# Attention stage: the bonus summed on TensorE, the gate in groups of four, and two ScalarE steps moved

## The chip, the cores and the metric

The kernel runs on one core of a Trainium2 chip. The metric is the device time of one execution in microseconds; times are given as the median of several runs, and one further execution was profiled.

## The reference

The program is a chain of three parts. Only the first is touched. It is linear attention with a decaying state and a bonus for the current token, for 4 batches, 8 heads, 768 tokens and a head width of 48:

```python
for t in range(S):
    kt, vt, rt = (k[:, :, t], v[:, :, t], r[:, :, t])
    cur = np.einsum('bhd,bhe->bhde', u[None] * kt, vt)
    y[:, :, t] = np.einsum('bhd,bhde->bhe', rt, state + cur)
    state = w[None, :, :, None] * state + np.einsum('bhd,bhe->bhde', kt, vt)
```

The term with `cur` is the bonus: for each token and head it is the number sum over d of r·u·k, times the row v. The 3072 rows of 384 values that come out are then multiplied by `w_gate` (384 x 8); these logits send each row to one of 8 experts with room for 384 rows each, by the order of all logits. Each expert applies two matrices, and a last part takes the maximum of three products and one more matrix.

## The kernel before

The attention is cut into 24 steps, one for each chunk of 128 tokens of one batch: step i works on batch i % 4 and chunk i // 4, so the state of a batch is needed again four steps later. The loop in `run` (L318 to L344) issues, for each i, the work of several steps at different distances, and every engine takes its own part of that order strictly in sequence:

- SP issues the loads of step i+4 (`load`: k, r and v in rows of tokens) and of step i+3 (`across`: r turned, as `rt`), and the store of the rows of step i-1.
- POOL multiplies `rt` by powers of the decay (`decayed`, L128), k by inverse powers (`natural`, L183, result `kp`), makes r·k and then r·k·u (`bonus`, L191 and L192, result `rk`), and after DVE has summed that over d (`extra`, L200, result `bon`) multiplies v by the sums (L202, result `bv`).
- PE turns `kp` of step i+2 (`turn`, L212, into the one buffer `pT`), multiplies it with `rt` for step i+1 (`scores`, L226, into `pA`), turns the output rows of step i-1 (`cross`, L297, into `pX`), runs four products of constants whose result nobody reads (`keep`, L236), forms the output of step i from the state and from the masked scores (`rows`, L247, into `pY`), multiplies the turned rows of step i-2 by the gate (`gate`, L307, into `lg`, where all logits stay until the loop ends), and forms the new state (`state`, L281, into `pK`).
- DVE masks the scores (L229, `am`), adds `bv` to the output (L262, `x`) and adds the old state (L285, `st`).
- ScalarE copies `pT` out (L214, `kt`) and `pX` (L299, `xt`), squares the rows of step i for a later scale (L263), and copies the new state back with its decay, in four instructions (L289, `S`).

Between these, at the places `side(1)` to `side(4)`, the loop runs items of a feed: pieces of preparing later weights, each a few instructions on DVE and ScalarE (squares L610, splits L677 and L681, bit work L717 to L748, splits L773 and L776), now and then a small product on PE. How many run at a place follows from fixed costs written in the code, and that list does not depend on the time. When the 24 steps are done, the logits are copied out (L352), and the routing begins with them.

Of the kernel before, what the change touches and what calls it, by code (L numbers as in the profile page):

```python
# [37 lines left out]
KEEP = 4  # L38
# [6 lines left out]
class Attention:  # L45


    def __init__(self, ctx, tc, K, r, rt, k, v, w, u, wg, x_dram, spare, routing):
        self.spare, self.routing = spare, routing
        self.tc, self.nc, self.K = tc, tc.nc, K  # L50
        self.r, self.rt, self.k, self.v, self.x_dram = r, rt, k, v, x_dram
# [4 lines left out]
        self.psum = ctx.enter_context(tc.tile_pool(name="psum_a", bufs=1, space=PSUM))  # L56
        self.steps = [(b, c) for c in range(NC) for b in range(B)]
        self.LD, self.RN, self.KN, self.BV, self.RT, self.KT, self.AM, self.X, self.XT, self.RK = ({} for _ in range(10))
        wcol = self.tabs.tile([128, NP], F32, name="wcol")
        nc.vector.memset(wcol, 1.0)  # L60
        for s in range(2):
            nc.sync.dma_start(wcol[HALF[s]], ap(w, s * D, [[1, D], [R2, NP]]))
        self.RB, self.KB, self.KP = ([self.tabs.tile([128, NP * C], F32, name=f"{name}{j}") for j in range(m)]
                                     for name, m in (("rt", 4), ("kt", 2), ("kp", 4)))
# [14 lines left out]
        self.ub = self.tabs.tile([128, DM], F32, name="ub")  # L79
        nc.sync.dma_start(self.ub, ap(u, 0, [[0, 128], [1, DM]]))  # L80
# [4 lines left out]
        self.wg = self.tabs.tile([128, 3, E], F32, name="wg")  # L85
        nc.sync.dma_start(self.wg, ap(wg, 0, [[E, 128], [128 * E, 3], [1, E]]))
# [3 lines left out]
        self.bonus(1)  # L90
        for i in range(2):
            self.decayed(i, nc.vector)
        self.bonus(0, nc.vector)
        self.fading()
        self.bank = self.psum.tile([128, 512], F32, name="lg")
        self.lg = self.bank[:, :NT * E].rearrange("p (m e) -> p m e", e=E)
        nc.tensor.matmul(self.bank[:, 256:], self.K.onesf.bitcast(BF16)[:, :128], self.K.onesf.bitcast(BF16), start=True, stop=True,
                         skip_group_check=True)
# [19 lines left out]
    def across(self, i):  # L118
# [3 lines left out]
        t = self.RT[i] = self.RB[i % 4]  # L122
# [62 lines left out]
    def bonus(self, i, engine=None):  # L185
        if i >= NT:
            return
        engine = engine or self.nc.gpsimd
        kn, rn, vn = self.LD[i]
        t = self.RK[i] = self.work.tile([128, DM], F32, name="rk")  # L190
        engine.tensor_mul(t, rn, kn)  # L191
        engine.tensor_mul(t, t, self.ub)  # L192

    def extra(self, i):
# [7 lines left out]
        nc.gpsimd.tensor_mul(bv.rearrange("p (h d) -> p h d", h=H), vn.rearrange("p (h d) -> p h d", h=H),  # L202
# [3 lines left out]
    def turn(self, i):  # L206
# [3 lines left out]
        pk = psum.tile([128, 512], F32, name="pT")  # L210
# [20 lines left out]

    def keep(self, n):

        ones = self.K.onesf.bitcast(BF16)
        for _ in range(n):
            self.nc.tensor.matmul(self.bank[:, 256:], ones[:, :128], ones, start=False, stop=True, skip_group_check=True)  # L236

    def rows(self, i):
# [24 lines left out]
        nc.scalar.activation(self.K.junk[:, :DM], x, AF.Square, accum_out=self.K.norms[:, i:i + 1])  # L263
# [7 lines left out]
    def state(self, i):  # L271
# [16 lines left out]
        for j in range(NP):  # L288
            nc.scalar.activation(S[:, j, :D], t[:, j, :D], AF.Copy, scale=self.w128[:, j:j + 1])  # L289

    def cross(self, i):
# [6 lines left out]
        xt = self.XT[i] = work.tile([128, 3, C], F32, name="xt", bufs=3)  # L298
        nc.scalar.activation(xt, px, AF.Copy)  # L299

    def gate(self, i):
        if i < 0:
            return
        b, c = self.steps[i]
        m = b * NC + c
        for j in range(3):
            self.nc.tensor.matmul(self.lg[:, m, :], self.XT[i][:, j, :], self.wg[:, j, :],  # L307
                                  start=(i == 0 and j == 0), stop=j == 2, skip_group_check=True)

    def run(self, feed):  # L310
# [40 lines left out]
        K = self.K  # L351
        nc.scalar.activation(K.raw, self.lg, AF.Copy, scale=-1.0)  # L352
# [1064 lines left out]
def body(ctx, tc, r, rt, k, v, w, u, wg, w1, w2, v1, v2, v3, wo, out, dbg=None):  # L1417
# [14 lines left out]
    with ExitStack() as actx:  # L1432
        A = Attention(actx, tc, K, r, rt, k, v, w, u, wg, x_dram,
# [11 lines left out]
_INS = ['r', 'rt', 'k', 'v', 'w', 'u', 'moe_w_gate', 'moe_w1', 'moe_w2', 'moe2_w1', 'moe2_w2', 'moe2_w3', 'moe2_w_out']  # L1445
# [3 lines left out]
def layout(inputs):  # L1449
# [5 lines left out]
    for name in _INS:  # L1455
        if name == "rt":
            a = inputs["r"].reshape(B, NP, 2, NC, C, D).transpose(0, 3, 2, 5, 1, 4)
        elif name in "rkv":
            a = inputs[name].transpose(0, 2, 1, 3)
        else:  # L1460
            a = inputs[name]
# [25 lines left out]
```

## Time and profile before

| | us |
|---|---|
| median of 3 runs (lowest, highest) | 698.33 (697.42, 699.98) |
| the profiled execution | 696.23 |
| its span, first to last instruction | 694.5 |

Over the whole span PE is busy 93%, DVE 58%, ScalarE 51% and POOL 34%. The page cuts the span in 40 slices of 17.4 us; a digit is the busy share in tenths. POOL's line is 6999999960050003..., so POOL is full from the second to the eighth slice, and this is the attention: its loop ends at 160.5 us. The granted clock of TensorE (line PEclk, tenths of full speed) is 8999999995579999: near full in the attention, lower in the routing that follows, and full in the experts.

A busy PE in these views is a modelled figure: records of products overlap, and each lasts longer than the time to the next. The distance between the starts of neighbouring groups is therefore read, not their length.

### The profile page before, as it was taken

The numbers are of one execution on the slowest core, as the hardware profiler recorded it, in microseconds if no ns is written. First come the engines' busy times: TensorE is split into PE (matmuls) and PEld (weight loads), VectorE is DVE, ScalarE is ACT, GpSimd is POOL, SyncE is SP. The second block draws the span as 40 slices with busy tenths as digits, with TensorE's granted clock in tenths as the row PEclk, the third lists the DMA queues.
The fourth block names the chain that finished last, engine by engine and source line by source line (L and its number), as shares of the span: only waits on it lengthen the run. The fifth ranks groups of instructions, "written<-read, shape, count | busy, mean of one in ns | idle before, by whom it ended". The sixth has DMA issues, their size and how long they took to land.

```text
span 694.5 us, 14402 instructions
## 1 busy us (share of the span) xinstructions
PE 644.6 (93%) x5663; PEld 427.2 (62%) x5663; DVE 400.7 (58%) x1068; ACT 351.5 (51%) x785; POOL 238.0 (34%) x264
## 2 busy tenths in 40 slices
PE   7999998996599998699999999999999999999996
PEld 5788777875476554356666656666665666666663
DVE  7778897776725867646466455644636553451321
ACT  3766657643425556367466547446365536342321
POOL 6999999960050003113022112102212111110222
PEclk8999999995579999899999999999999999999999
DMA  7996757513034516016235211620612220000000
GB/s 220 315 295 216 246 186 250 162 37 103 2 107 139 172 42 194 22 68 160 68 103 108 98 57 30 170 75 35 160 45 74 45 89 1 35 0 1 36 1 34
DMA packets 54762, 72.97 MB, mean 105 GB/s; under 512 B 21408, under 2 KB 42016, under 8 KB 54688
## 3 DMA queue, kind: packets, MB, share of 16 engines
q1 hardware_dynamic: 51616, 62.55, 29.3%
q0 software_dynamic: 3072, 9.44, 4.7%
q8 instruction: 46, 0.75, 0.5%
q14 instruction: 28, 0.23, 0.1%
HBM read 58.41 MB, written 9.44 MB: 98 GB/s over the span
## 4 chain that ended last, share of the span: by engine, by line
PE 54%; issue 8%; DVE 5%; ACT 4%; POOL 1%; POOLq 0%; DVEq 0%; ACTq 0%
PE pg L897 25%; PE ps L897 20%; PE px L990 8%; ACT w L677 1%; DVE top L972 1%; POOL gt L977 1%; ACT junk L610 1%; DVE da L739 1%; DVE x2s L953 0%; ACT gt L976 0%; DVE ht L925 0%; DVE v L776 0%; DVE sc L423 0%; DVE da L732 0%; POOL out_dram L995 0%
## 5 line engine op out<-in xcount | busy, mean ns | idle before, releaser
L897 PE MATMUL pg<-x2s,v 128*128 128x384 f16 x1296 | 218.2, 326 | 5.3 <-ACT top L970 3.2
L897 PEld LDWEIGHTS <-v 128*128 128x128 f16 x1296 | 126.6, 98 | 90.9 <-issue 6.0
L977 POOL TENSOR_TENSOR gt<-top,gt 128x384 f16<-128x384 f32 x48 | 44.5, 928 | 349.2 <-ACT gt L976 295.5
L897 PEld LDWEIGHTS <-w 128*128 128x128 f16 x1242 | 116.8, 98 | 73.7 <-issue 2.3
L681 DVE SCALAR_TENSOR_TENSOR w<-stage,sc,w 128x512 f16<-128x512 f32 (+1 forms) x80 | 70.9, 906 | 61.1 <-ACT w L677 60.9
L972 DVE SCALAR_TENSOR_TENSOR top<-pg,sc,top 128x384 f32<-128x384 f32 x96 | 59.1, 615 | 74.4 <-PE pg L897 63.6
L897 PE MATMUL ps<-ht,w 128*128 128x384 f16 x576 | 94.9, 326 | 1.6 <-DVE ht L925 1.6
L897 PE MATMUL ps<-xt,w 128*128 128x384 f16 (+1 forms) x540 | 88.4, 317 | 0.2 <-ACT xt L888 0.2
L990 PE MATMUL px<-wo,gt 128*128 128x384 f16 x432 | 75.0, 334 | 6.9 <-DVE wo L776 3.0
L976 ACT ACTIVATE gt<-top 128x384 f16<-128x384 f32 x48 | 25.1, 523 | 109.5 <-DVE top L972 109.5
L990 PEld LDWEIGHTS <-gt 128*128 128x128 f16 x432 | 42.7, 100 | 38.1 <-issue 8.8
L677 ACT ACTIVATE w<-stage,sc 128x512 f16<-128x512 f32 (+1 forms) x80 | 61.6, 798 | 2.2 <-DVE sc L461 2.2
L610 ACT ACTIVATE junk<-stage 128x768 bf16<-128x768 f32 x64 | 53.7, 838 | 0.9
L925 DVE SCALAR_TENSOR_TENSOR ht<-ps,ht 128x384 f16<-128x384 f32 x56 | 31.0, 555 | 32.1 <-ACT ht L924 32.1
L995 POOL DMA_INDIRECT out_dram<-o,ids x24 | 23.9, 996 | 46.7 <-ACT o L993 46.7
L970 ACT ACTIVATE top<-pg,sc 128x384 f32<-128x384 f32 x48 | 27.6, 576 | 20.8 <-PE pg L897 18.3
L263 ACT ACTIVATE junk<-x 128x384 bf16<-128x384 f32 x24 | 12.6, 524 | 47.0 <-DVE x L262 44.7
L936 ACT ACTIVATE x<-ps 128x384 f32<-128x384 f32 x24 | 11.7, 490 | 47.0 <-PE ps L897 47.0
L924 ACT ACTIVATE ht<-ps 128x384 f16<-128x384 f32 x56 | 26.8, 482 | 15.9 <-PE ps L897 15.7
L993 ACT ACTIVATE o<-px,sc 128x384 f32<-128x384 f32 x24 | 13.9, 580 | 38.8 <-PE px L990 35.5
L229 DVE TENSOR_TENSOR am<-pA,mask 128x512 f32<-128x512 f32 x48 | 30.7, 681 | 4.3 <-PE pA L226 4.2
L128 POOL TENSOR_TENSOR rt<-rt,tr 128x512 f32<-128x512 f32 x22 | 31.4, 1427 | 0.2 <-DMA rt<-in_rt_dram 0.2
(231 smaller groups left out, 884.3 us busy)
## 6 DMA issues: line engine op xcount, KB each, us to landing
stage<-in_moe_w_dram SPq DMA_DIRECT2D x41, 768.0 KB, 5.6
kn<-in_k_dram SPq DMA_DIRECT2D x24, 192.0 KB, 4.9
rn<-in_r_dram SPq DMA_DIRECT2D x24, 192.0 KB, 5.0
v<-in_v_dram SPq DMA_DIRECT2D x24, 192.0 KB, 4.0
rt<-in_rt_dram SPq DMA_DIRECT2D x48, 96.0 KB, 3.5
x_rows<-x SPq DMA_DIRECT2D x24, 192.0 KB, 2.9
stage<-in_moe_w_out_dram SPq DMA_DIRECT2D x3, 768.0 KB, 4.4
xg<-x_rows,ids POOLq DMA_INDIRECT x24, 4.6
```

The costliest lines, as they stand in the source:

```text
L128: (engine or self.nc.gpsimd).tensor_mul(self.RT[i], self.RT[i], self.tr)
L229: nc.vector.tensor_mul(am[:, s], pa[s], self.mask[:, None, :].to_broadcast([128, NP, C]))
L610: self.nc.scalar.activation(self.K.junk, x, AF.Square, accum_out=total)
L677: nc.scalar.activation(hi, raw, AF.Copy, scale=st["s"])
L681: nc.vector.scalar_tensor_tensor(lo, raw, st["s"], hi, op0=OP.mult, op1=OP.subtract)
L897: nc.tensor.matmul(p[:, rows], w[:, wi, k, cols], x[:, xi, k, rows], start=k == 0 and wi + xi == 0, stop=k == kb - 1 and xi == 1, skip_gro ...
L924: nc.scalar.activation(h[:, 0, f], p, AF.Relu)
L925: nc.vector.scalar_tensor_tensor(h[:, 1, f], p, 0.0, h[:, 0, f], op0=OP.max, op1=OP.subtract)
L970: nc.scalar.activation(t, p, AF.Copy, scale=self.ratio[i])
L972: nc.vector.scalar_tensor_tensor(t, p, self.ratio[i], top, op0=OP.mult, op1=OP.max)
L977: nc.gpsimd.tensor_sub(gt[:, 1, g], top, gt[:, 0, g])
L990: nc.tensor.matmul(p, gt[:, gi, g, a * 128:(a + 1) * 128], self.WO[:, wi, g, :], start=g == 0 and gi + wi == 0, stop=g == self.KG - 1 and ...
```

## The change

1. **Bonus on TensorE.** r is no longer loaded in rows, and `bonus` goes with its two products on POOL. `product(i+2)` multiplies on DVE the turned k in `pT` (PSUM) by `rt`; `tally(i+1)` sums that over d on PE, with a weight of 32 columns (`uw`, holding u·w in two columns, zeros in the rest), four products with 128 columns of moving data into four groups of 32 output rows, and ScalarE copies the 128 x 128 result (`ts`). `extra(i+1)` turns the sums with a product of `ts` and columns of the identity (8 columns), ScalarE copies these 8 columns (`bon`), and POOL multiplies v by them as before. DVE's reduction is gone. `rt` has five buffers, `bv` three.
2. **Gate in fours.** For the steps up to 19 the three products of each step (weight: the turned rows; moving: 8 columns of the gate) become, once in four steps, 12 products with a weight of 32 columns (8 of the gate, the rest zero) and 128 columns of moving data into four groups of 32 rows, a ScalarE copy (`gs`), and one step later one product that turns the result and a ScalarE copy to `raw`. The last four steps keep the old form.
3. **No products of constants.** `keep` is removed, with its first product ahead of the loop.
4. **ScalarE's order.** The Square of the rows moves from `rows(i)` to `cross(i-1)`, behind the copy `xt`. The four state copies become `fade(i-1)`, behind `turn(i+2)` and its copy `kt`, and ahead of `tally(i+1)`'s copy. `side(2)` now stands behind `tally`.

The core of the diff:

```diff
-        for name, src in (("kn", self.k), ("rn", self.r), ("vn", self.v)):
+        for name, src in (("kn", self.k), ("vn", self.v)):
...
-    def bonus(self, i, engine=None):
+    def product(self, i):
+
         if i >= NT:
             return
-        engine = engine or self.nc.gpsimd
-        kn, rn, vn = self.LD[i]
-        t = self.RK[i] = self.work.tile([128, DM], F32, name="rk")
-        engine.tensor_mul(t, rn, kn)
-        engine.tensor_mul(t, t, self.ub)
+        t = self.PR[i] = self.work.tile([128, NP * C], F32, name="pr")
+        self.nc.vector.tensor_mul(t, self.PK, self.RT[i])
+
+    def tally(self, i):
+
+        if i >= NT:
+            return
+        nc = self.nc
+        for j in range(NP):
+            nc.tensor.matmul(self.sums[32 * j:32 * j + 32], self.uw[:, j], self.PR[i][:, j * C:(j + 1) * C], start=True, stop=True,
+                             skip_group_check=True)
+        t = self.TS[i] = self.work.tile([128, C], F32, name="ts")
+        nc.scalar.activation(t, self.sums, AF.Copy)
 
     def extra(self, i):
         if i >= NT:
             return
         nc, work = self.nc, self.work
-        vn = self.LD[i][2]
+        nc.tensor.matmul(self.weights, self.TS[i], self.four[:, :, :2], start=True, stop=True, skip_group_check=True)
         s = work.tile([128, H], F32, name="bon")
-        nc.vector.tensor_reduce(s, self.RK[i].rearrange("p (h d) -> p h d", h=H), AX.X, OP.add)
-        bv = work.tile([128, DM], F32, name="bv")
+        nc.scalar.activation(s, self.weights, AF.Copy)
+        bv = work.tile([128, DM], F32, name="bv", bufs=3)
...
-        nc.scalar.activation(self.K.junk[:, :DM], x, AF.Square, accum_out=self.K.norms[:, i:i + 1])
...
-        for j in range(NP):
-            nc.scalar.activation(S[:, j, :D], t[:, j, :D], AF.Copy, scale=self.w128[:, j:j + 1])
+        self.ST[i] = t
+
+    def fade(self, i):
+        if i in self.ST:
+            for j in range(NP):
+                self.nc.scalar.activation(self.S[self.steps[i][0]][:, j, :D], self.ST[i][:, j, :D], AF.Copy,
+                                          scale=self.w128[:, j:j + 1])
...
-        xt = self.XT[i] = work.tile([128, 3, C], F32, name="xt", bufs=3)
+        xt = self.XT[i] = work.tile([128, 3, C], F32, name="xt", bufs=6)
         nc.scalar.activation(xt, px, AF.Copy)
+        nc.scalar.activation(self.K.junk[:, :DM], self.X[i], AF.Square, accum_out=self.K.norms[:, i:i + 1])
+
+    def gates(self, c):
+
+        nc = self.nc
+        for j in range(3):
+            for b in range(B):
+                nc.tensor.matmul(self.across_logits[32 * b:32 * b + 32], self.wg[:, j], self.XT[c * B + b][:, j],
+                                 start=j == 0, stop=j == 2, skip_group_check=True)
+        t = self.GS = self.work.tile([128, C], F32, name="gs", bufs=1)
+        nc.scalar.activation(t, self.across_logits, AF.Copy)
+
+    def logits(self, c):
+        self.nc.tensor.matmul(self.lg, self.GS, self.four[:, :, :E], start=True, stop=True, skip_group_check=True)
+        self.keep(c)
...
+    def keep(self, c):
+        self.nc.scalar.activation(self.raw[:, :, c], self.lg.rearrange("p (b e) -> p b e", e=E), AF.Copy, scale=-1.0)
...
         for i in range(2):
             self.turn(i)
+            self.product(i)
         self.scores(0)
+        self.tally(0)
         self.extra(0)
...
             self.natural(i + 3)
-            self.bonus(i + 2)
             side(1)
             self.turn(i + 2)
+            self.fade(i - 1)
+            self.tally(i + 1)
             side(2)
             self.scores(i + 1)
-            self.extra(i + 1)
+            self.product(i + 2)
             side(3)
             self.cross(i - 1)
-            self.keep(KEEP)
+            self.extra(i + 1)
             self.rows(i)
-            self.gate(i - 2)
+            if i > B and i % B == 2:
+                self.logits(i // B - 1)
+            if i > B and i % B == 1:
+                self.gates(i // B - 1)
+            if i - 2 >= NT - B:
+                self.gate(i - 2)
             side(4)
             self.state(i)
```

## Rows read from the trace of the kernel before

**Rows 1.** Busy time by stretch: start:end, length, engines with instruction counts, clock, DMA

```profile
49.00:114.00 65.00, 60.27 (x1147) 51.44 (x1144) 57.17 (x99) 39.50 (x104) 64.22 (x51) 0.97 0.70 227
114.00:142.00 28.00, 28.00 (x551) 24.04 (x551) 18.65 (x45) 19.31 (x54) 27.61 (x26) 1.00 0.54 166
```

**Rows 2.** POOL's groups, 20 to 143 us: count, busy us, mean ns, idle before

```profile
L128 POOL TENSOR_TENSOR rt<-rt,tr 128x512 f32<-128x512 f32 x20 | 28.4, 1420 | 0.2 <-DMA rt<-in_rt_dram 0.2
...
L183 POOL TENSOR_TENSOR kp<-kn,tkn 128x384 f32<-128x384 f32 x21 | 25.0, 1192 | 0.0
...
L192 POOL TENSOR_TENSOR rk<-rk,ub 128x384 f32<-128x384 f32 x21 | 24.7, 1176 | 1.6
...
L191 POOL TENSOR_TENSOR rk<-rn,kn 128x384 f32<-128x384 f32 x21 | 24.1, 1146 | 0.0
...
L202 POOL TENSOR_TENSOR bv<-v,bon 128x384 f32<-128x384 f32 x20 | 22.2, 1111 | 0.0
```

**Rows 3.** PE's timeline, one step that waits for nobody: start us, length us

```profile
125.71 0.66 PE L212 MATMUL pT<-identf,kp 128*128 128x128 f32 x4
126.29 1.16 PE L226 MATMUL pA<-rt,kt 64*128 64x128 f32 x16
127.39 0.55 PE L297 MATMUL pX<-identf,x 128*128 128x128 f32 x3
127.77 0.60 PE L236 MATMUL lg<-onesf 128*128 128x256 bf16 x4
128.30 0.69 PE L247 MATMUL pY<-S,rt 64*64 64x64 f32 x32
128.93 1.15 PE L247 MATMUL pY<-v,am 128*64 128x64 f32 x32
130.01 0.83 PE L307 MATMUL lg<-wg,xt 128*128 128x8 f32 x6
130.77 0.69 PE L281 MATMUL pK<-v,kp 128*64 128x64 f32 x16
131.39 0.33 PE L212 MATMUL pT<-identf,kp 128*128 128x128 f32 x1
```

**Rows 4.** Waits, 20 to 150 us: who for whom, us in total, times, longest

```profile
PE pT L212 <- POOL kp L183: 6.0, 7, 1.6
...
ACT junk L263 <- DVE x L262: 42.0, 22, 4.5
```

**Rows 5.** PE's timeline at the lower clock, after a wait for POOL, as rows 3

```profile
74.39 1.11 PE L212 MATMUL pT<-identf,kp 128*128 128x128 f32 x4 [1.61 <-POOL kp L183]
75.43 2.08 PE L226 MATMUL pA<-rt,kt 64*128 64x128 f32 x16
```

**Rows 6.** ScalarE's timeline, start us, length us: state copies, kt, xt

```profile
51.71 1.01 ACT L289 ACTIVATE S<-st,w 128x48 f32<-128x48 f32 x4 [1.68 <-DVE st L285]
52.63 0.57 ACT L214 ACTIVATE kt<-pT 128x512 f32<-128x512 f32 x1
53.10 0.47 ACT L299 ACTIVATE xt<-pX 128x384 f32<-128x384 f32 x1
```

**Rows 7.** One small copy of the routing: ns least/median/most, first and last start

```profile
L1198 ACT ACTIVATE seen<-pc x3: 167/167/168, 162.1 to 177.8; 96x1 f32<-96x1 f32 x3
```

**Rows 8.** DVE's groups of the attention and one feed line, 20 to 143 us, as rows 2

```profile
L229 DVE TENSOR_TENSOR am<-pA,mask 128x512 f32<-128x512 f32 x40 | 25.6, 681 | 3.7 <-PE pA L226 3.7
...
L262 DVE TENSOR_TENSOR x<-pY,bv 128x192 f32<-128x192 f32 x42 | 13.0, 348 | 4.2 <-POOL kp L183 2.1 <-POOL rt L128 1.5 <-PE pY L247 0.4
...
L200 DVE TENSOR_REDUCE bon<-rk 128x8 f32<-128x384 f32 x21 | 11.3, 540 | 0.0
...
L776 DVE SCALAR_TENSOR_TENSOR v<-wo,sc,v 128x768 f16<-128x768 f32 x6 | 8.7, 1446 | 1.6 <-ACT v L773 1.6
...
L285 DVE TENSOR_TENSOR st<-pK,S 128x192 f32<-128x192 f32 x16 | 5.6, 347 | 1.1 <-PE pK L281 1.1
```

**Rows 9.** That feed line over the whole span: ns least/median/most, first and last start

```profile
L776 DVE SCALAR_TENSOR_TENSOR v<-wo,sc,v x9: 1012/1089/2099, 93.5 to 252.8; 128x768 f16<-128x768 f32 x9
```

More of the change, by code (lines that the diff above doesn't have):

```diff
@@ L56, in __init__ @@
         self.psum = ctx.enter_context(tc.tile_pool(name="psum_a", bufs=1, space=PSUM))
+        self.ST = {}
         self.steps = [(b, c) for c in range(NC) for b in range(B)]
-        self.LD, self.RN, self.KN, self.BV, self.RT, self.KT, self.AM, self.X, self.XT, self.RK = ({} for _ in range(10))
+        self.LD, self.RN, self.KN, self.BV, self.RT, self.KT, self.AM, self.X, self.XT, self.PR, self.TS = ({} for _ in range(11))
         wcol = self.tabs.tile([128, NP], F32, name="wcol")
         nc.vector.memset(wcol, 1.0)
+        ucol = self.tabs.tile([128, NP], F32, name="ucol")
         for s in range(2):
@@ L63, in __init__ @@
         self.RB, self.KB, self.KP = ([self.tabs.tile([128, NP * C], F32, name=f"{name}{j}") for j in range(m)]
-                                     for name, m in (("rt", 4), ("kt", 2), ("kp", 4)))
+                                     for name, m in (("rt", 5), ("kt", 2), ("kp", 4)))
         self.S = [self.tabs.tile([128, NP, WIDE], F32, name=f"S{b}") for b in range(B)]
@@ L78, in __init__ @@
         self.routing.fill()
-        self.ub = self.tabs.tile([128, DM], F32, name="ub")
-        nc.sync.dma_start(self.ub, ap(u, 0, [[0, 128], [1, DM]]))
+        for s in range(2):
+            nc.sync.dma_start(ucol[HALF[s]], ap(u, s * D, [[1, D], [R2, NP]]))
+        self.uw = self.tabs.tile([128, NP, 32], F32, name="uw")
+        nc.gpsimd.memset(self.uw, 0.0)
         self.load(1)
@@ L84, in __init__ @@
         self.across(2)
-        self.wg = self.tabs.tile([128, 3, E], F32, name="wg")
-        nc.sync.dma_start(self.wg, ap(wg, 0, [[E, 128], [128 * E, 3], [1, E]]))
+        self.wg = self.tabs.tile([128, 3, 32], F32, name="wg")
+        nc.gpsimd.memset(self.wg, 0.0)
+        nc.sync.dma_start(self.wg[:, :, :E], ap(wg, 0, [[E, 128], [128 * E, 3], [1, E]]))
         self.tables(wcol)
@@ L89, in __init__ @@
         self.natural(2)
-        self.bonus(1)
         for i in range(2):
             self.decayed(i, nc.vector)
-        self.bonus(0, nc.vector)
+        for s in range(2):
+            nc.vector.tensor_mul(self.uw[HALF[s], :, s], ucol[HALF[s]], wcol[HALF[s]])
         self.fading()
         self.bank = self.psum.tile([128, 512], F32, name="lg")
-        self.lg = self.bank[:, :NT * E].rearrange("p (m e) -> p m e", e=E)
-        nc.tensor.matmul(self.bank[:, 256:], self.K.onesf.bitcast(BF16)[:, :128], self.K.onesf.bitcast(BF16), start=True, stop=True,
-                         skip_group_check=True)
+        self.across_logits, self.sums = self.bank[:, :C], self.bank[:, C:2 * C]
+        self.weights, self.lg = self.bank[:, 2 * C:2 * C + H], self.bank[:, 3 * C:3 * C + 4 * E]
+        self.raw = self.K.raw.rearrange("p (b c) e -> p b c e", b=B)
+        self.four = self.K.identf.rearrange("p (g n) -> p g n", n=32)
     def clear(self, t):
@@ L230, in scores @@
         self.AM[i] = am
[L232 to L236, printed above, removed]
     def rows(self, i):
@@ L350, in run @@
         self.gate(NT - 1)
-        K = self.K
-        nc.scalar.activation(K.raw, self.lg, AF.Copy, scale=-1.0)
+        self.keep(NC - 1)
 class Consts:
@@ L1416, in body @@
 @with_exitstack
-def body(ctx, tc, r, rt, k, v, w, u, wg, w1, w2, v1, v2, v3, wo, out, dbg=None):
+def body(ctx, tc, rt, k, v, w, u, wg, w1, w2, v1, v2, v3, wo, out, dbg=None):
     nc = tc.nc
```

26 lines of the change are left out of this document (11 added, 15 removed).

## The prediction

> **What bounds the kernel now.** Only the attention is touched, so I looked at its stretch first, by engine, in two parts: 49 to 114 us, where the feed works on the bit pieces, and 114 to 142 us. A step holds 113 records of products on PE (4, 16, 3, 4, 32, 32, 6 and 16) [rows 3], so the first part is 1147 / 113 = 10.15 steps of 6.40 us, the second 551 / 113 = 4.88 steps of 5.74 us [rows 1]. POOL is busy 64.22 of 65 and 27.61 of 28 us: it never rests. PE, though, is busy all 28 us of the second part as well, and 60.27 of the first.
>
> The groups of POOL say what fills it: 1.420 + 1.192 + 1.176 + 1.146 + 1.111 = 6.05 us a step with next to no idle time [rows 2]. PE's timeline of a step without a wait gives the second limit: from turn to turn 131.39 - 125.71 = 5.68 us, each group following the one before at once [rows 3]. So POOL's 6.05 and PE's 5.68 lie close together, and POOL leads where it is stretched. The waits agree: PE stood 6.0 us in 7 waits for POOL's `kp` [rows 4]. One of them was followed by a fall of the granted clock to 1.2 GHz, at which the turn took 1.11 us for 0.66 and the scores 2.08 for 1.16, 1.4 us together [rows 3, 5]. ScalarE's 42.0 us behind DVE's `x` [rows 4] are idle time of an engine that no one waits for.
>
> To be read from this: taking POOL's load away is worth its waits, some 7 us, and no more; what decides is what PE's own step becomes.
>
> **POOL.** It loses 1.176 + 1.146 us of 6.05, and keeps 3.72 us a step: off the path, also with the wait for `bon` in front of `bv`, behind which the next step's `rt` and `kp` are queued (2.6 us, while their readers on PE are over a step away). Gain: 6.0 of waits and 1.4 of clock, 7.4 us.
>
> **PE's step.** One 128-column pass of these f32 products costs 0.11 us: the scores, 16 records two at a time, take 1.10 us to the next group's start, of which about 0.2 is the last pass and a change of array shape (8 x 0.11 + 0.2). A change of shape alone costs about 0.09 (from the end of a pass at 0.11 to a start at 0.2).
> - Removed: the constants, 128.30 - 127.77 = 0.53, and the gate, 130.77 - 130.01 = 0.76 [rows 3].
> - `tally`: four f32 products are 8 records. Where four column groups run at once, as the 64 x 64 quarters of `pY<-S` do (32 records in 0.63 us, 0.02 each), it is 2 x 0.11 and a change of shape: 0.31. If no two overlap, 8 x 0.11 + 0.09 = 0.97.
> - the product that turns `ts`: two records of the gate's kind, 0.76 - 4 x 0.11 = 0.32.
> - gate in fours: 24 records, 6 x 0.11 + 0.09 = 0.75 and its turning 0.32, over four steps 0.27. With no overlap (24 x 0.11 + 0.09 + 0.32) / 4 = 0.76.
>
> The sum is 5.68 - 0.53 - 0.76 + 0.31 + 0.32 + 0.27 = 5.29 us, 0.39 less; over 23 steps 9.0 us. I take the overlap, because two halves (`pY<-v`: 32 records in 1.08 us) and four quarters both show it [rows 3]; two at a time would cost 0.22 + 0.17 more a step, and no overlap 0.66 + 0.49 = 1.15 more. The Trainium skill, page "TensorEngine Tiling (Array Packing)", section "Tiling Modes", lists 128 x 32 as four independent tiles, but page "TensorE: Matmul & The Clock Gate", section "Part 3: Packing small matmuls", reports 2.38 times the speed for three column tiles; no run here shows either. By that share of full overlap the two groups would cost about a quarter more, an estimate of 0.1 us a step, and the time would be 2 us longer.
>
> **The new wait.** The turning of `ts` stands in the same step as `tally`, and on ScalarE `ts` stands behind `kt` and the four state copies. Queued on PE behind it: the output of step i, the state, and the next turn. From the turn's start, PE reaches it after 0.58 + 0.31 + 1.10 + 0.38 = 2.37 us [rows 3]. ScalarE can begin `kt` when the turn ends, 0.66; the next instruction starts 0.47 later (53.10 - 52.63), the four state copies take 0.92 (52.63 - 51.71) [rows 6], and `ts`, 128 columns, lies between the 0.167 us of a few columns [rows 7] and `xt`'s 0.47 for 384 [rows 6]; I take 0.27, nearer to the small one. That is 0.66 + 0.47 + 0.92 + 0.27 = 2.32, and some 0.1 for two signals: PE waits about 0.1 a step, 2 us over 20 steps. The ends are nothing, and 0.6 a step if feed pieces at `side(4)` and `side(1)` (0.8 to 0.9 each) still hold ScalarE when the turn ends. `bon` needs 0.17 and only POOL waits for it. Square moves unchanged; it now reads rows that are a step old, so the 42 us of waits go, and gain nothing by themselves. Behind the last `xt` it lies beside the last gate (0.76); uncovered it would cost half a microsecond once.
>
> **DVE.** It loses the sum, 0.540, and gains `product`, the same shape from PSUM as the mask, 0.681 [rows 8]. In the first part it is busy 57.17 / 10.15 = 5.63 us a step [rows 1]: its own 2 x 0.681 + 2 x 0.348 + 0.540 + 0.347 = 2.95, so 2.68 of feed. After: 3.09 and 2.68, 5.77, if the feed keeps its length. But feed instructions are stretched there: 1.446 us on average in the attention for 1.012 at best, with a longest of 2.099, while the mask does not move [rows 8, 9]. If POOL's missing third frees them wholly, 2.68 x 0.70 = 1.88 and 4.97 a step. Page "SBUF — State Buffer", section "Who interferes with whom" of the Trainium skill, says that a DVE instruction with two SBUF inputs and a GpSimd one that reads SBUF shut each other out for a whole instruction; the rows agree for both sorts of DVE instruction, and by that rule the stretch shrinks as POOL's share does, by about a third, to 5.5 a step. I take 5.7, because the new state is added behind the feed of `side(4)`, and the state copies, `ts` and PE now follow it: 0.3 over PE's 5.39, for 10.15 steps 3 us. The ends: nothing, and 0.5 a step.
>
> **The rest.** SP loses a load of each step and nothing moves past another; POOL hardly ever waits for a load (0.2 us [rows 2]), so I cost this at nothing. Start: DVE drops two products and makes two of 0.68, PE gets a tally and its turning, and the second turn also waits for `product(0)`; no change, within 2 us either way. Later stages are not touched.
>
> **Sum.** 7.4 + 9.0 - 2 - 3 = 11.4 us. The profiled execution took 696.23 us (span 694.5), so 684.8 (span 683.1); it ran 2.1 us under the median of 698.33, on whose scale the forecast is 687.0.
>
> **Rivals.**
> - *PE alone sets the pace.* Neither `ts` nor DVE is ever late and the start gains 2: 7 us more, 680. For: the wait is of the size of its uncertainty. Against: DVE's 5.63 a step.
> - *The new wait takes the gain.* ScalarE or DVE come to `kt` and the state copies late in every step, 0.6 us each: 20 x 0.5 more than I took, 697, no change. For: PE, ScalarE and DVE now close a ring in one step, and ScalarE's feed pieces stand ahead of `kt`. Against: ScalarE has 39.50 us of work in 65.
> - *The column groups don't overlap.* PE's step is 5.29 + 1.15 = 6.44; PE then arrives later than `ts`, so no wait, and DVE is no bound: 23 x 1.15 = 26 more, less 5: 708, slower. It decides from about 0.5 us a step; two at a time gives 687 + 9 - 2 = 694.
> - *The clock.* Without the constants TensorE falls to 1.2 GHz more often. Each such stretch cost 1.4 us here; ten of them end at 701. Against: the one fall stood behind a wait of 1.61 us [rows 5], and these go.
>
> That the change does not do what it says would show as POOL still full.
>
> **How the numbers follow.** Forecast 0.56 (682 to 694, two at a time included), PE alone 0.15, the wait 0.15, no overlap 0.09, the clock 0.05. About 0.5%, 3.5 us, is what a measurement tells from no change: faster is below 694.8, slower above 701.8. Faster: forecast and PE alone, 0.71, and of the wait and clock cases 0.04: 0.75. Same: 0.14 of those two. Slower: 0.09 and 0.02. The range leaves out the no-overlap case and some of the edges: 677 to 701.
>
> **What would show it.** POOL's groups at 3.5 to 3.8 us a step; the tally's 8 records two rounds of 0.11 apart; turn to turn on PE 5.3 to 5.5 where the feed is light, 5.7 where it is heavy; `ts` about 0.27; a short wait of PE for `ts`; clock 1.0 up to the end of the loop; feed lines of DVE nearer to their best. Wrong if PE waits over half a microsecond a step for `ts`, or if the tally's records stand 0.11 apart.

## The result, and the profile after

| | before | after |
|---|---|---|
| median (lowest, highest), us | 698.24 (697.42, 699.98) | 709.42 (704.25, 711.07) |
| the profiled execution | 696.23 | 709.59 |
| output of step 0 begins on PE | 19.0 | 24.8 |
| last logits copied to `raw`, the loop's end | 160.4 | 173.3 |
| from there to the end of the span | 534.1 | 534.5 |

The changed kernel is slower, where 11 us faster had been forecast: the medians differ by 11.2 us, and the recorded ratio of the runs is 1.0125 (95% interval 1.0093 to 1.0158), which is 8.7 us. The last line says where not to look: everything behind the attention takes the same time. The loss of 12.9 us in the profiled execution lies in the start (5.8) and in the loop (148.5 for 141.4 us, 7.1).

First the two lines of the changed kernel's page with POOL's busy tenths and the granted clock, 17.7 us a slice.

```profile
POOL 5554546550031003213113102302311111210222
...
PEclk7789899999558999989999999999999999999998
```

POOL, which was full before, is now half busy. Its three groups in the loop (24 to 168 us; columns as in [rows 2]):

```profile
L133 POOL TENSOR_TENSOR rt<-rt,tr 128x512 f32<-128x512 f32 x21 | 29.2, 1389 | 1.3 <-DMA rt<-in_rt_dram 1.3
...
L188 POOL TENSOR_TENSOR kp<-kn,tkn 128x384 f32<-128x384 f32 x21 | 27.4, 1307 | 4.5 <-PE pK L288 3.9 <-POOL rt L133 0.6
...
L216 POOL TENSOR_TENSOR bv<-v,bon 128x384 f32<-128x384 f32 x23 | 19.5, 848 | 62.9 <-ACT bon L214 60.3 <-DMA rt<-in_rt_dram 2.6
```

That is 1.389 + 1.307 + 0.848 = 3.54 us a step, and 62.9 us in which POOL waits in front of `bv`, 60.3 of them for `bon`: the bound of [rows 2] is gone. PE's own step is shorter too. Its timeline from one turn to the next in a step where PE stands for nobody (columns as in [rows 3]):

```profile
101.54 0.66 PE L226 MATMUL pT<-identf,kp 128*128 128x128 f32 x4
102.13 0.43 PE L203 MATMUL lg<-pr,uw 128*32 128x128 f32 x8
102.48 0.38 PE L439 MATMUL pX<-sc,onesf 1*128 1x1 f32 x2
102.79 1.16 PE L240 MATMUL pA<-rt,kt 64*128 64x128 f32 x16
103.88 0.55 PE L309 MATMUL pX<-identf,x 128*128 128x128 f32 x3
104.27 0.29 PE L212 MATMUL lg<-identf,ts 128*128 128x8 f32 x2
104.48 0.69 PE L255 MATMUL pY<-S,rt 64*64 64x64 f32 x32
105.11 1.15 PE L255 MATMUL pY<-v,am 128*64 128x64 f32 x32
106.09 0.64 PE L288 MATMUL pK<-v,kp 128*64 128x64 f32 x16
106.66 0.55 PE L226 MATMUL pT<-identf,kp 128*128 128x128 f32 x3
```

It takes 5.12 us, a feed product of 0.31 (L439) included and no gate, which now comes in every fourth step; [rows 3] had 5.68. So both things that the change set out to do are done. What eats them stands in the waits (20 to 165 us; us in total, times, longest us):

```profile
POOL bv L216 <- ACT bon L214: 62.2, 22, 6.1
PEld lg L212 <- ACT ts L206: 16.4, 12, 3.4
...
ACT junk L645 <- DVE wo L783: 8.8, 4, 4.7
...
ACT S L300 <- DVE st L292: 4.5, 5, 1.4
```

PE waits 16.4 us, 12 times, for ScalarE's copy `ts`; the 6.0 us for `kp` of [rows 4] are gone. POOL's 62.2 us cost next to nothing: the same view has 1.9 us in which PE waits behind them. The last piece is the granted clock. Stretches of the loop and, below them, those at half speed (start:end, length, busy us of PE, PEld, DVE, ACT, POOL with counts, granted clock, DMA share, GB/s):

```profile
24.80:60.00 35.20, 30.46 (x546) 25.74 (x545) 24.85 (x50) 24.09 (x75) 18.80 (x17) 0.85 0.63 203
60.00:130.00 70.00, 59.59 (x1225) 49.06 (x1221) 60.24 (x103) 45.34 (x136) 38.31 (x32) 0.95 0.57 181
130.00:173.40 43.40, 40.76 (x861) 34.72 (x861) 27.70 (x62) 26.86 (x84) 16.57 (x16) 0.96 0.34 106
```

```profile
7.80:28.30 20.50, 15.84 (x130) 12.71 (x130) 12.01 (x18) 4.96 (x13) 9.58 (x10) 0.50 0.57 170
38.50:45.30 6.80, 6.80 (x62) 5.71 (x63) 2.45 (x9) 4.73 (x15) 3.01 (x3) 0.50 0.56 167
82.90:89.70 6.80, 5.73 (x104) 5.02 (x106) 3.92 (x8) 3.41 (x12) 2.06 (x2) 0.50 0.26 96
130.70:134.10 3.40, 3.40 (x66) 3.16 (x66) 0.08 (x1) 1.73 (x6) 2.05 (x2) 0.50 0.56 210
```

0.50 is 1.2 of 2.4 GHz. The start stays there until 28.3 us (before: 16.4), and three more falls lie in the loop, 17.0 us together, for one of 3.4 before.

Two places show how the time goes. First a step with a long wait, all engines (start us, length us, in brackets the idle time before and what ended it):

```profile
125.00 2.04 DVE L783 SCALAR_TENSOR_TENSOR wo<-stage,da 128x768 int32<-128x768 int32 x1
...
125.61 0.66 PE L226 MATMUL pT<-identf,kp 128*128 128x128 f32 x4
...
126.19 1.72 POOL L188 TENSOR_TENSOR kp<-kn,tkn 128x384 f32<-128x384 f32 x1
...
127.14 0.84 ACT L645 ACTIVATE junk<-wo 128x768 bf16<-128x768 f32 x1 [3.05 <-DVE wo L783]
...
127.65 0.55 PE L309 MATMUL pX<-identf,x 128*128 128x128 f32 x3
...
128.10 0.84 ACT L645 ACTIVATE junk<-stage 128x768 bf16<-128x768 f32 x1
...
128.95 0.58 ACT L228 ACTIVATE kt<-pT 128x512 f32<-128x512 f32 x1
129.42 1.00 ACT L300 ACTIVATE S<-st,w 128x48 f32<-128x48 f32 x4
...
130.32 0.26 ACT L206 ACTIVATE ts<-lg 128x128 f32<-128x128 f32 x1
...
130.63 0.49 PEld L212 LDWEIGHTS lg<-identf,ts 128*128 128x128 f32 x2 [2.68 <-ACT ts L206]
```

Read it from the bottom. PE waits 2.68 us for `ts`. In ScalarE's queue ahead of it stand the four state copies, ahead of them `kt`, and ahead of `kt` two Squares of the feed, the first of which waited 3.05 us for a feed instruction of DVE that took 2.04 us. The turn was over at 126.27 (125.61 + 0.66); `kt` began at 128.95. In the step before, `kt` began at 121.10, ahead of PE's scores at 121.35, and PE waited 0.37. Behind the wait shown the clock falls at 130.7. The fall at 82.9 lies inside the longest wait for `ts`, 3.41 us up to 83.97. The fall at 38.5 stands behind another wait of PE, for the copy of `pX`:

```profile
38.30 0.08 PEld L433 LDWEIGHTS pX<-identf,sc 128*1 128x1 f32 x1 [1.69 <-ACT xt L311]
```

There `xt` stood behind a Square of the feed that had waited 1.71 us for its load from memory: the same queue, another copy.

Second the start, PE alone:

```profile
11.98 1.06 PE L226 MATMUL pT<-identf,kp 128*128 128x128 f32 x4
16.14 1.08 PE L226 MATMUL pT<-identf,kp 128*128 128x128 f32 x4 [3.10 <-DVE pr L195]
17.15 2.08 PE L240 MATMUL pA<-rt,kt 64*128 64x128 f32 x16
...
24.80 1.44 PE L255 MATMUL pY<-v,am 128*64 128x64 f32 x22
```

The second turn stands 3.10 us for `product(0)`, which reads the only `pT`; then everything up to 24.80 runs at the low clock (scores 2.08 us as in [rows 5], not 1.16). What `product(0)` waits for shows in DVE's queue (and ScalarE's `kt`) in the same stretch:

```profile
11.88 2.29 DVE L133 TENSOR_TENSOR rt<-rt,tr 128x512 f32<-128x512 f32 x2 [0.63 <-ACT tr L174]
...
13.08 0.60 ACT L228 ACTIVATE kt<-pT 128x512 f32<-128x512 f32 x1 [1.23 <-PE pT L226]
...
14.09 1.12 DVE L97 TENSOR_TENSOR uw<-ucol,wcol 48x4 f32<-48x4 f32 x2
...
15.30 0.68 DVE L195 TENSOR_TENSOR pr<-pT,rt 128x512 f32<-128x512 f32 x1
```

`kt` was done at 13.68. DVE never rests between these lines: it first scales `rt` of the first two steps, then builds the new weight `uw` (1.12 us), and comes to the product at 15.30.

### The profile page after: what moved, and what is told of

Its sections match the earlier page's. It is cut to its first block, busy times and chain, and to the rows that moved or that the text cites. A ratio compares the mean times of both kernels' runs of the same rounds, so it can differ in the third digit from the quotient of the medians.

```text
span 707.8 us, 14729 instructions
## 1 busy us (share of the span) xinstructions
PE 646.5 (91%) x5816; PEld 426.2 (60%) x5816; DVE 402.3 (57%) x1068; ACT 359.2 (51%) x843; POOL 182.3 (26%) x221
## 4 chain that ended last, share of the span: by engine, by line
PE 53%; issue 7%; DVE 5%; ACT 3%; POOL 1%; POOLq 0%; DVEq 0%; ACTq 0%
PE pg L932 25%; PE ps L932 20%; PE px L1025 8%; ACT w L712 1%; DVE top L1007 1%; POOL gt L1012 1%; ACT junk L645 1%; DVE da L774 1%; DVE x2s L988 0%; ACT gt L1011 0%; DVE ht L960 0%; DVE v L811 0%; DVE sc L458 0%; DVE da L767 0%; PE px L914 0%
## 5 line engine op out<-in xcount | busy, mean ns | idle before, releaser
L716 DVE SCALAR_TENSOR_TENSOR w<-stage,sc,w 128x512 f16<-128x512 f32 (+1 forms) x80 | 71.4, 918 | 57.8 <-ACT w L712 57.8
L960 DVE SCALAR_TENSOR_TENSOR ht<-ps,ht 128x384 f16<-128x384 f32 x56 | 30.9, 554 | 32.2 <-ACT ht L959 32.1
L216 POOL TENSOR_TENSOR bv<-v,bon 128x384 f32<-128x384 f32 x24 | 20.3, 847 | 69.0 <-ACT bon L214 66.4
L1005 ACT ACTIVATE top<-pg,sc 128x384 f32<-128x384 f32 x48 | 27.6, 576 | 20.5 <-PE pg L932 18.1
L243 DVE TENSOR_TENSOR am<-pA,mask 128x512 f32<-128x512 f32 x48 | 30.7, 680 | 11.4 <-PE pA L240 11.2
L959 ACT ACTIVATE ht<-ps 128x384 f16<-128x384 f32 x56 | 26.8, 482 | 15.9 <-PE ps L932 15.6
L188 POOL TENSOR_TENSOR kp<-kn,tkn 128x384 f32<-128x384 f32 (+1 forms) x25 | 31.4, 1260 | 8.8 <-ACT tkn L172 4.3
```

Source lines behind the costliest of these rows:

```text
L188: self.nc.gpsimd.tensor_mul(self.KN[i][:, heads, :D], kn[:, heads], self.tkn[:, heads, :D])
L243: nc.vector.tensor_mul(am[:, s], pa[s], self.mask[:, None, :].to_broadcast([128, NP, C]))
L716: nc.vector.scalar_tensor_tensor(lo, raw, st["s"], hi, op0=OP.mult, op1=OP.subtract)
L959: nc.scalar.activation(h[:, 0, f], p, AF.Relu)
L960: nc.vector.scalar_tensor_tensor(h[:, 1, f], p, 0.0, h[:, 0, f], op0=OP.max, op1=OP.subtract)
L1005: nc.scalar.activation(t, p, AF.Copy, scale=self.ratio[i])
```

## The experiments

The theory after the result: `ts` is late because of what stands ahead of it in ScalarE's queue. The rivals: the feed's Square that waits for DVE is the real cause and was hurting before; the clock fell because the constants left; the start alone makes the loss. Unless said otherwise an experiment is the changed kernel with the edit shown. Ratios are to the kernel before, which was run again beside each group of experiments (medians 698.2 to 699.7). Differences in us are between medians of different groups, so some 1.5 us of one can be that.

**The tally first.** `tally`, and with it `ts`, goes ahead of the feed place `side(1)`, the turn, `kt` and the state copies.

```diff
+            self.tally(i + 1)
             side(1)
             self.turn(i + 2)
             self.fade(i - 1)
-            self.tally(i + 1)
```

> The changed kernel, with tally(i+1) and its ScalarE copy issued ahead of side(1) and of the turn, so that ts stands before kt and the four state copies. In the changed kernel PE waited 16.4 us for ts, and the granted clock lay at 1.2 GHz from 38.5 to 45.3, 82.9 to 89.7 and 130.7 to 134.1 us. If ScalarE's queue in front of ts is the cause (queue theory), the waits fall below 5 us, the falls of the clock inside the loop mostly go with them, and the time is 8 to 13 us below the changed kernel's 709.4: 697 to 701. If the missing constants let the clock fall by themselves (clock theory), the falls stay and the time is 705 or more. The later start (output of step 0 at 24.8 us for 19.0) stays by either.

Measured: 697.35 us (692.66 to 700.67), ratio 0.9973 (0.9938 to 1.0008): 12.1 us less than the changed kernel. Its line of PE's wait for `ts`, 15 to 175 us:

```profile
PEld lg L212 <- ACT ts L206: 0.9, 1, 0.9
```

The wait for `ts` is all but gone; PE now waits 4.4 us for DVE's product and 4.2 for `bon`, which it had not before. One of the three falls in the loop is left (79.9 to 86.7 us). The start is as late as before the edit (25.2 us).

**The feed's Square later.** In the feed, the Square of a piece that DVE has just signed moves behind the next piece's work.

```diff
-                if early:
-                    total(j - 1)
...
-                if not early:
-                    total(j - 1)
+                total(j - 1)
```

> The changed kernel, with the feed's Square of the bit pieces one feed item later, so that ScalarE does not stand behind the DVE instruction that writes its input (8.8 us in 4 waits in the changed kernel, and kt, the state copies and ts are queued behind it). Queue theory: PE's waits for ts in the steps from 76 to 131 us shrink by 5 to 8 us, and one or both falls of the clock there go: 700 to 704. If the chain kt, state copies, ts is too long by itself, without the feed in front of it, the waits of about 1.0 to 1.4 us stay in these steps: 707 to 710. Clock theory: unchanged within 2 us.

Measured: 699.58 us (697.82 to 703.5), 1.0011 (0.9981 to 1.0041). ScalarE's wait for DVE's `wo` fell from 8.8 to 1.8 us, but PE's wait for `ts` hardly did:

```profile
PEld lg L212 <- ACT ts L206: 14.7, 13, 2.3
```

So of the 9.8 us won, most came another way: the output of step 0 began at 22.6 (2.2 sooner), and the loop has 6.8 us of low clock for 20.5. The start is not touched by the edit; in this execution it had the low clock from 9.1 to 12.5 and 15.9 to 19.3 us only. The longest wait is 2.3 for 3.4. This run doesn't separate the Square's part from the clock's.

**The constants back.** Four products of constants a step, 96 columns each, between `cross` and `extra`.

```diff
+            ones = self.K.onesf.bitcast(BF16)
+            for _ in range(4):
+                nc.tensor.matmul(self.bank[:, 416:], ones[:, :128], ones[:, :96], start=True, stop=True, skip_group_check=True)
```

> The changed kernel with four products of constants a step between cross and extra (96 columns of moving data each), just ahead of the place where PE waits for ts. Clock theory: the falls of the clock inside the loop go, 5 to 7 us faster, 702 to 704. Queue theory: the constants lie inside the wait where there is one and cost 0.4 us in the about 10 steps without one, the long waits and the falls behind them stay: 708 to 713.

Measured: 707.44 us (704.36 to 710.65), 1.0113 (1.0041 to 1.0186). Two of the falls come at nearly the same places (columns as above):

```profile
36.90:43.70 6.80, 6.80 (x61) 5.64 (x61) 2.66 (x9) 4.84 (x16) 3.01 (x3) 0.50 0.56 155
81.20:88.10 6.90, 5.50 (x100) 4.80 (x101) 4.25 (x8) 3.27 (x13) 2.05 (x2) 0.51 0.31 111
```

The third fall, at 130 us, isn't there. Products of constants in PE's stream wait when the stream waits (10.8 us of the wait for `ts` now stand in front of them), so they do not fill the gap. At this place they do not keep the clock up, and the time is that of the changed kernel within the noise.

**A warm start.** Products of constants in the gaps of the start: 14 behind the first turn, 4 behind the first tally.

```diff
             self.product(i)
+            if i == 0:
+                idle = self.psum.tile([128, 512], F32, name="pX")
+                warm(nc, self.K, idle, 14)
...
         self.tally(0)
+        warm(nc, self.K, idle, 4)
```

> The changed kernel with 14 products of constants between the first and the second turn of the start, where PE waits for DVE's first product, and 4 more behind the first tally. In the changed kernel the clock lies at 1.2 GHz from 7.8 to 28.3 us, in the kernel before from 9.5 to 16.4. If the later start (5.8 us up to the output of step 0) is the clock's, it returns by about 18 us and the time is 3 to 4 us lower, 705 to 706; the rest of the 5.8 us is the second turn's wait for DVE's product. If the whole start is that wait, the time does not change.

Measured: 701.27 us (698.49 to 705.68), 1.0031 (0.9996 to 1.0065). The stretch that had stood at 0.50:

```profile
7.80:28.30 20.50, 17.98 (x239) 14.41 (x241) 15.02 (x25) 9.42 (x28) 11.20 (x12) 1.00 0.72 217
```

The second turn still starts at 16.15, yet the output of step 0 at 21.2: 3.6 of the 5.8 us. That the clock is at full speed from 7.8 on, ahead of the first added product (12.84), is not the edit's doing: in the four later kernels with the same products it stood at 0.50 for 3.4 to 6.8 us between 7.5 and 15.0, but not behind that. Without them six kernels had it there up to 19.3 to 28.9. The output of step 0 began at 20.7 to 21.6 with them, 22.6 to 25.2 without. In the two profiled executions the loop is also 6.2 us shorter, though PE's wait for `ts` stayed at 14.5 us: of the three falls only the one at 75.2 to 82.0 was there. Why the waits at 36 and 130 us were followed by a fall in the one kernel and not in the other stays open.

**These three together.**

> The changed kernel with three edits at once: tally and its copy ahead of the turn (12 us by itself), the feed's Square one item later (10 us) and the products of constants in the start (8 us). If the three causes are separate (ScalarE's queue in front of ts, its stand behind DVE, the start), the gains add up to some 25 us less an overlap of the first two, which shorten the same waits: 684 to 690, faster than the kernel before, and near the 687 of the forecast. If they are one cause, the clock that falls behind any wait, each edit alone has already taken most of it and the sum stops at 694 to 698.

Measured: 695.27 us (692.88 to 699.81), 0.9951 (0.9931 to 0.9971). Alone they won 12.1, 9.8 and 8.1 us, together 14.1. They are not three separate shares of the loss; the account below shows the clock as the part that they share.

**ScalarE's old order.** The changed kernel with the Square of the rows back in `rows(i)` and the state copies back in `state(i)`.

```diff
-            self.fade(i - 1)
...
+        nc.scalar.activation(self.K.junk[:, :DM], x, AF.Square, accum_out=self.K.norms[:, i:i + 1])
...
+        self.fade(i)
```

> The changed kernel with ScalarE's Square and state copies put back to where the kernel before has them (behind the output and the new state of step i); all else as changed. ts then has only kt ahead of it in its own step, but the Square waits for DVE's x and the copies for DVE's st, a step's end earlier in the queue. If the 0.92 us of state copies between kt and ts are what makes ts late, this is faster than the changed kernel, 700 to 704. If it is the waiting of ScalarE for DVE, the old order adds waits in front of kt, and it is no faster, 707 to 715.

Measured: 718.26 us (715.31 to 720.05), 1.0272 (1.0243 to 1.0302), 8.8 us worse than the changed kernel and beyond both expectations. Its waits:

```profile
ACT junk L271 <- DVE x L270: 43.9, 22, 3.8
PEld lg L212 <- ACT ts L206: 23.7, 19, 2.4
```

The 44 us of ScalarE behind `x`, which cost nothing before [rows 4], now stand ahead of `ts` and cost. The fourth part of the change is what makes the first bearable; it doesn't go far enough.

**The gate alone.** The kernel before with the gate in fours and without the constants, POOL's work as it was.

> The kernel before with the gate in fours and without the constants, nothing else: PE's step is about 5.68 - 0.53 - 0.76 + 0.27 = 4.66 us, POOL's 6.05 stays. If POOL's 6.05 bounds the kernel before, PE only waits more, about 0.4 us of each lighter step is won at most: 694 to 698. If the clock needs the constants, the longer waits let it fall several times, 1.4 us or more each: 700 to 708.

Measured: 700.2 us (699.18 to 705.75), 1.001 (0.999 to 1.003). PE has less to do and waits longer for POOL, 23.8 us where the kernel before has 7.2 (15 to 175 us, this kernel and below it the one before):

```profile
PEld pT L214 <- POOL kp L185: 23.8, 16, 3.5
```

```profile
PEld pT L212 <- POOL kp L183: 7.2, 8, 1.7
```

POOL is busy 69.14 of the 70 us from 60 to 130. So POOL did set the pace before, as read from [rows 2]. The clock, though, fell four times in the loop, 3.4 us each, for once before, and its mean over the ten executions is 0.948, for 0.959 in the kernel before beside it. The time lies in the second expected range, that of a clock which falls more often. This run doesn't tell the lack of the constants from the longer waits; the account below does so in part.

**The Square later, in the kernel before.** The second edit on the kernel before.

> The kernel before with the feed's Square one item later, the edit that took 10 us off the changed kernel. If that gain came from the new place of ts behind ScalarE's queue, there is nothing to win here, where nobody on PE waits for ScalarE: 697 to 700. If the Square's wait costs time whatever stands behind it, 690 to 695.

Measured: 699.75 us (697.58 to 701.92), 1.0005 (0.9987 to 1.0024). The Square's place costs the kernel before nothing. It costs something only where a copy that PE needs at once stands behind it.

**One line.** The changed kernel with the tally ahead of the four state copies, still behind `kt` and the feed.

```diff
             self.turn(i + 2)
-            self.fade(i - 1)
             self.tally(i + 1)
+            self.fade(i - 1)
```

> The changed kernel with one line moved: the copy ts ahead of the four state copies, still behind kt. This leaves out of ts's queue the 0.92 us of copies and their wait for DVE's st, and nothing else. If these copies are the main part of the queue, most of the 12 us of the early tally returns: 698 to 702. If kt and the feed in front of it hold ts, little returns: 705 to 709.

Measured: 697.18 us (693.15 to 700.27), 0.9973 (0.9952 to 0.9994): 12.2 us less than the changed kernel (10.6 by the ratios), as much as the larger move won. Its waits:

```profile
PE pT L226 <- DVE pr L195: 5.8, 3, 3.4
PEld lg L212 <- ACT ts L206: 5.6, 5, 2.5
```

The state copies between `kt` and `ts`, 0.92 us and their own wait for `st`, were so the greater part of the wait, 10.8 of the 16.4. ScalarE's wait for DVE's `wo` is unchanged (8.9 us), and the longest wait for `ts` that remains stands behind it (ScalarE's feed Square, then PE):

```profile
79.68 0.84 ACT L645 ACTIVATE junk<-wo 128x768 bf16<-128x768 f32 x1 [4.71 <-DVE wo L783]
...
81.32 0.30 PEld L212 LDWEIGHTS lg<-identf,ts 128*128 128x128 f32 x2 [2.51 <-ACT ts L206]
```

The start is as late as in the changed kernel (24.8), and one fall is left in the loop (39.1 to 45.9).

**The product first.** The three edits, and `product(i+2)` right behind the turn, so that `pT` comes free sooner.

> The three edits, and DVE's product issued right behind the turn, ahead of the masks of the scores. In the run with the three edits PE's tally, now the first work of a step, waited 4.1 us in 4 waits for that product and the turn 1.9 once more, while DVE stood 7.8 us for the scores. If DVE's place for the product is what is left, 690 to 693; if DVE is simply full where the feed is heavy, the waits move to the masks and the output and the time stays at 694 to 696.

Measured: 696.34 us (694.37 to 700.31), 0.9962 (0.9944 to 0.9981): nothing won. DVE now waits in front of the product, 7.3 us for `kt` and 5.9 for `rt`.

**The clearing later.** That kernel, with the clearing of the fifth `rt` buffer moved behind the tables of the start.

> As e9_product_first, with the clearing of the fifth rt buffer (0.52 us on POOL) moved from the front of POOL's queue into a stretch in which POOL idles. The tables of the start, which stood 0.7 us later in the changed kernel than before, come back by 0.5 us; the time falls by 0.5 us, or by more where the clock's step up comes earlier with it; at most 2 us less than e9_product_first.

Measured: 695.5 us (693.23 to 697.36), 0.9945 (0.9923 to 0.9967); the output of step 0 begins at 21.2 for 21.6. Half a microsecond of the start, less than the medians can tell.

**Four edits.** The one line, the Square later, the warm start and the clearing later.

> The changed kernel with ts ahead of the state copies, the feed's Square one item later, the products of constants in the start and the later clearing. The first edit took 12 us off alone, the second 10, the third 8. If they shorten different waits, 685 to 690; if the first two shorten the same waits of PE and the rest is DVE's load where the feed is heavy (what the run with the three edits, 695.3, points to), 692 to 696.

Measured: 695.24 us (692.17 to 698.02), 0.9961 (0.9942 to 0.998). That is 14 us under the changed kernel and 3 under the one before. The runs do not tell it from the three edits (0.9951) or from the clearing later (0.9945). Its stretch where the feed is heavy:

```profile
45.00:110.00 65.00, 57.14 (x1279) 48.26 (x1279) 59.64 (x105) 45.27 (x138) 41.83 (x32) 1.00 0.64 210
```

DVE is busy 59.64 of 65 us here, where [rows 1] had 57.17, at a full clock and with hardly a wait for `ts` left (1.4 us in all).

## Why the prediction was wrong, and where it was right

This is an account by single profiled executions. The loop runs from the first output of step 0 to the last copy to `raw`; low clock is the time in it at 1.2 GHz. At that clock PE's groups take close to twice as long [rows 3, 5], so low clock costs at most half its length; the last column takes that half off.

| kernel | start | loop | low clock in it | PE waits for `ts` | loop less half the low clock |
|---|---|---|---|---|---|
| before | 19.0 | 141.4 | 3.4 | none | 139.7 |
| after | 24.8 | 148.5 | 20.5 | 16.4 | 138.3 |
| warm start | 21.2 | 142.3 | 6.8 | 14.5 | 138.9 |
| Square later | 22.6 | 141.7 | 6.8 | 14.7 | 138.3 |
| one line | 24.8 | 138.6 | 10.9 | 5.6 | 133.2 |
| tally first | 25.2 | 136.1 | 10.3 | 0.9 | 131.0 |

Among the changed kernels the last column falls with the wait for `ts`, within a microsecond, as it should if wait and clock are the two causes. By it the change itself gains 8.7 us in the loop (139.7 - 131.0, with the tally first as the change without its wait), the wait takes 7.3 of them back (138.3 - 131.0), and the clock takes 8.6 (half of 20.5 - 3.4). The sum, 7.2 lost in the loop and 5.8 in the start, must come out at the 12.9 to be explained, since the column is made from the loop and the low clock; what the table tells is the split.

How firm the split is can be read from the clock of the executions that were not profiled, whose mean is on record too. Half speed loses half of its time, so (1 - mean clock) x span is the most that the clock can have cost in an execution, over the whole span. Averaged over the executions it is 28 to 30 us for the kernel before (four groups), 39.1 for the changed one, 34.2 for the tally first, 35.1 for the one line, 32.1 for the Square later, 31.6 for the warm start and 30.7 for the three edits. So the clock takes some 10 us of the loss, where the two profiled executions have 14.7, and the split is good to about 5 us. Nearly all that the Square later and the warm start won is clock (7.0 and 7.5 us); of what the tally first and the one line won it is 4 to 5. Alone the three edits save 4.9, 7.0 and 7.5 us of clock, together 8.4: this is the part that doesn't add up.

- **POOL, right.** 3.54 us a step, inside the 3.5 to 3.8 that were to show it, and no wait for `kp` where PE was held before. The gate alone shows that POOL had been the limit.
- **PE's step, right.** Without the feed product of 0.31 and with a quarter of the gate (0.27) the 5.12 us are 5.08, for a forecast of 5.29. The four column groups run at once: of the tally's eight records four start within 0.02 us and the other four 0.11 later, and from its start to the next group's pass 0.35 us, where one pass at a time would need 0.97. The Trainium skill, page "TensorEngine Tiling (Array Packing)", section "Tiling Modes", counts 128 x 32 as four independent tiles; the trace agrees. The 0.1 us a step that a partial overlap would have added isn't to be seen. The rival without overlap falls.
- **Prices of single copies, right.** `ts` took 0.267 us for the 0.27 taken, `bon` 0.172 for 0.17, the product 0.678 for 0.681.
- **The new wait, wrong; this is the step that failed.** PE's wait for `ts` was put at 0.1 us a step, 2 us in the sum, from the sentence that ScalarE can begin `kt` when the turn ends. It was 16.4 us. In four of the 12 waits (8.6 us) ScalarE could not begin `kt`, because a Square ahead of it waited for DVE's `wo`; in five (5.4 us) the state copies behind `kt` waited for DVE's `st`; the other three (2.4 us) have neither. The upper end of 0.6 a step was of the true size (16.4 / 23 = 0.7), and its reason, pieces of the feed that hold ScalarE, was the true one in part. The four state copies were in the sum with their 0.92 us, which made ScalarE's 2.32 as long as PE's 2.37, so that every delay ahead of `ts` counted; that they wait for `st`, and need not stand there, was missed: one line moved wins 12 us. The wait should have been costed with what every instruction ahead of `ts` waits for, not only with its length. The sign that the prediction set for this, over half a microsecond a step, is what the waits show.
- **The rival that has this wait, right in kind, too cheap.** It gave 697, the loss of the expected gain and no more. Two things that it left out, 5.8 us of the start and the 8.6 of the clock in the loop (an upper price), make the difference to 709.4; that the sum closes so well is partly luck, since the rival took 12 us for the wait where the table gives 7.3, and a larger gain than there was.
- **The clock, wrong.** The forecast had it at 1.0 to the end of the loop. The rival about the clock was right that falls would be more, 20.5 us of low clock for 3.4 in the loop. It priced a fall at 1.4 us; two of the three here last 6.8, up to 3.4 each. Its reason, the missing constants, is not what the traces show. In the 14 profiled kernels the clock fell 26 times between 20 and 157 us, each time in a wait of PE of 1.45 us or more, or up to 2.2 us behind one: in the changed kernel 3.17 us around 82.9, 2.44 ahead of 130.7, 1.55 for `xt` ahead of 38.5 (PE's own idle time; its weight load stood a little longer, as in the lines above). There were 50 such waits, so a wait isn't always followed by a fall; what decides stays open. With constants in PE's stream (the kernel before, the Square later in it, the constants back) 4 of 7 were followed by one, without them 22 of 43. So the change lost the clock by its new waits, as far as these few counts tell.
- **The start, wrong.** "Within 2 us either way" was 5.8. The second turn's wait for `product(0)` was named, and its length not worked out: the product stood in DVE's queue behind the scaling of `rt` and the new `uw`, so that the second turn began at 16.14 for 12.45 before, 3.7 of the 5.8. The rest came behind it, at the low clock up to 28.3 us; the warm start gives 3.6 of the 5.8 back, though its second turn begins no sooner.
- **DVE, half right.** The added work is as costed, but the relief of the feed did not come. Its four groups with two inputs take 42.0 us in the loop for 41.8 before (the splits, L716, 17.9 for 17.3; L811 8.7 for 8.7; L783 7.7 for 7.3; L774 7.7 for 8.5); the line of [rows 9], now L811, took 1.478 us on average for 1.446 [rows 8]. Only the group with a single input, L767, came down, 5.1 for 6.2. The prediction expected these lines nearer to their best, and by POOL's share about a third off their stretch, 5.5 us a step; the forecast's own 5.7 was close to the 5.77 without any relief. The Trainium skill, page "SBUF — State Buffer", section "Who interferes with whom", has a DVE instruction with two SBUF inputs contend with a GpSimd one that reads SBUF, over ports that are an exclusive lock; the two long ones in the step shown (2.04 on DVE beside 1.72 on POOL) agree, but that the stretch shrinks with POOL's share was my step, and the trace does not bear it out. With the four edits the feed-heavy steps take 6.1 us (some 119 records of PE a step: 1279 / 119 = 10.7 steps in 65 us), for 5.7 forecast and 6.40 before. Whether DVE alone holds them there was not separated.
- **The rest, right.** 534.5 us behind the loop for 534.1; the load that SP lost shows no price (POOL's waits for `rt`, 1.3 and 2.6 us, lie in time that it has to spare).

## What to carry to other kernels

Where a result goes from PE through ScalarE and back within one step, price everything that stands ahead of the copy in ScalarE's queue, and what each of those waits for; put the copy ahead of work that follows another engine, which here was one line and 12 us. An engine that is taken off the path exposes a ring of the others, and waiting there is paid a second time if TensorE's clock falls behind it. Edits that each remove such a wait do not add up: here 12.1, 9.8 and 8.1 us were 14.1 together.

## What the runs showed of the hardware that was not expected

- Two fifths of POOL's time freed (6.05 to 3.54 us a step) did not shorten DVE's two-input feed instructions beside it, 42.0 us in all for 41.8.
- Eight f32 products with 32-column weights in four column groups cost PE 0.35 us up to the next group, 0.04 a product; the 24 of the gate, 0.80 (76.67 to 77.47 us with the four edits).
- Products of constants at their place in PE's stream did not keep the clock up (two falls of 6.8 us with them). The same kind of products in the gaps of the start did: in five kernels no low clock between 15.0 and 28.3 us, where the changed kernel was at 0.50.
- The falls of the clock in the loop stand in or behind waits of PE, 26 of 26, but of the 50 waits counted above only 26 have a fall.
